# Attention scan and bilinear feed-forward on one core: pair 1's x, Wb's second piece and two first products change their places

## The chip, the cores and the metric
The kernel runs on one core of a Trainium2 chip. Five engines work side by side, each through its own list of instructions: TensorE (PE; its weight loads are shown as PEld), VectorE (DVE), ScalarE (ACT), GpSimd (POOL) and SyncE (SP). Transfers between memory and the on-chip buffer are issued by SP, ACT or GpSimd and carried by 16 DMA engines that all issuers share. The metric is the device time of one execution in microseconds (us), lower is better.

## The reference
First stage: for each of 4 batches x 8 heads a recurrent scan over 768 tokens, done in chunks of 32, with head size 32 and state size 16:

```
la  = log(clip(a)); cum = cumsum(la)              # in a chunk
M   = (C B^T) * exp(cum_i - cum_j) * causal
y   = M x  +  (C state) * exp(cum_i)
state = exp(sum la) * state + sum_j B_j x_j * exp(cum_last - cum_j)
```

Second stage, over the 3072 tokens with the heads side by side (256 wide):

```
out = ((y @ w_a) * (y @ w_b)) @ w_out             # w_a, w_b: 256 x 1536, w_out: 1536 x 256
```

Inputs and output are float32.

## The kernel before
The tokens of a batch are cut into 6 blocks of 128. A **pair** is one block of two batches, so there are 12 pairs; pairs 0 and 1 are the first block of all four batches. For a pair, B and C are scaled by decay factors (`scale_bc`), turned (`transposes`), and multiplied head by head (`scores`); the products are masked to the causal part (`mask`), x is scaled to float16 (`scale_x`), and `pv` or `pv_u` multiplies the masked products with x and so makes the scan's output y for this pair, laid into `X2T`. The feed-forward follows: products of `X2T` with Wa go to banks called `aps`, products with Wb to banks called `bps`, ACT copies `aps` out (`evac_a`), DVE multiplies both (`times`), and the product with Wo makes the output. Two pairs of the first blocks are done one after the other; later blocks take both pairs at once.

Wa and Wb are each 256 rows by 1536 columns. They are kept in two tiles by column half (index 0 and 1), and each tile has two pieces by row half, `f`. `load_w(W, t, f)` loads one piece; `load_w(W, t)` loads both. A GpSimd transfer turns float32 to float16 on its way. All weight loads are issued by GpSimd.

Every engine works its list strictly in the written order, since the kernel is scheduled by hand; semaphores for the data are put in by the framework. So the order of lines in the file is the order of each engine's work, and the order of a queue's issues is that of its transfers.

At the start, SP loads `a` and parts of pair 0's inputs, ACT other parts of them. GpSimd makes two masks by `affine_select`, then issues (L213 to L220) B and C of pair 1 in two halves each (`bt` 0 and 1), Wa's two pieces of columns 0, the second half of pair 1's x, and Wb's two pieces of columns 0. The first half of pair 1's x is issued by SP (L203) and held behind the reciprocal `f0` (L761, L762), so that it stays behind pair 0's x; the constant `c32` follows it on SP (L204).

From L757 on the compute: `warmup` products keep TensorE busy while data are on the way, DVE makes the decay factors of pair 0, TensorE its transposes and scores, DVE its four masked products. GpSimd scales B and C of pair 1 (L778, L783), then issues the second column halves of Wa and Wb (L784, L785), and makes `causal_q`, the mask for the later blocks (L786). On TensorE the order is: first half of pair 0's y (`pv_u(0, 0, ...)`, L792), the transposes of pair 1 (L795), second half of pair 0's y (L796), two first products with Wa of row half 0 (L801), the scores of pair 1 (L802), the other products of row half 0 (L804), those of row half 1 (L805), the products with Wb of row half 0 (L823), then `pv(1)` (L824) and the rest with Wb (L826, L827). ACT copies each half of pair 0's y out (`evac0`), the copies of row half 0 follow the first half, those of row half 1 the second. The helper `units_mm` (L625) holds the products with L628; its last arguments are the row half and which of the six products are done.

Psum banks are given out in the order of the calls of `bank` by the list `BANKS`; the first `aps` bank is one that nothing used before, the second and third are the two `py` banks of pair 0.

Of the kernel before, what the change touches and what calls it, by code (L numbers as in the profile page):

```python
# [14 lines left out]
ALU = mybir.AluOpType  # L15
PSUM = bass.MemoryType.PSUM
AFTER = mybir.DependencyInfo(mybir.DependencyClass.Sync, mybir.DependencyReason.DATA)
# [12 lines left out]
def kernel(  # L30
# [102 lines left out]
    def bank(name):  # L133
        return psf.tile([128, 512], f32, name=name, tag=f"ff{next(banks)}")
# [11 lines left out]
    def load1(eng, p, which, bt, i0=0, n=64):  # L146
        blk, bp = divmod(p, NBP)
        if p >= P0:
            return eng.dma_start(
                by_token(pair_in[p][which])[:, bt],  # L150
                (B, C, x)[which][2 * bp + bt, :, blk * Q : (blk + 1) * Q, :].rearrange("h q n -> q h n"),
            )
        src = (B, C, x)[which][2 * bp + bt, :, blk * Q + 2 * i0 : blk * Q + 2 * i0 + 2 * n, :]
        return eng.dma_start(
            pair_in[p][which][64 * bt + i0 : 64 * bt + i0 + n].rearrange("i h r n -> i h (r n)"),
            src.rearrange("h (i r) n -> i h (r n)", r=2),
        )
# [10 lines left out]
    def load_w(W, t, f=None):  # L168
        src = (moe_w_a if W is Wa else moe_w_b).rearrange("(f p) e -> p f e", p=128)[:, :, t * KC : (t + 1) * KC]
        fs = slice(0, 2) if f is None else slice(f, f + 1)  # L170
        return nc.gpsimd.dma_start(W[t][:, fs], src[:, fs])
# [28 lines left out]
    nc.vector.memset(hsx, 0.0)  # L200
    nc.vector.memset(causal_q, 1.0)
    nc.vector.memset(c32, 0.0)
    x1 = load1(nc.sync, 1, 2, 0)  # L203
    nc.sync.dma_start(c32[0:BH], p32_t.ap())  # L204
    nc.gpsimd.affine_select(
        out=ident, in_=ident, compare_op=ALU.is_equal, fill=0.0, base=0, pattern=[[-1, 128]], channel_multiplier=1
    )
# [7 lines left out]
            load1(nc.gpsimd, 1, w, bt)  # L215
    load_w(Wa, 0, 0)
    load_w(Wa, 0, 1)
    load1(nc.gpsimd, 1, 2, 1)
    load_w(Wb, 0, 0)
    load_w(Wb, 0, 1)  # L220

    def warmup(n, bank, reps=4):
        for _ in range(n):
# [83 lines left out]
    def scale_bc(p, which, eng, factor=None):  # L307
        blk, bp = divmod(p, NBP)
        name = ("bm", "cm")[which]
        if p >= P0:  # L310
            f = (fBl, fCl)[which][:, blk - P0 // NBP].rearrange("p (b t h) -> p b t h", b=NBP, t=2)[:, bp]
        else:
            f = (f_c(blk) if which else fB[:, blk])[:, :, bp]
        raw = by_token(pair_in[p][which]) if p >= P0 else pair_in[p][which].rearrange("p h r n -> p r h n")
        m_ = pre.tile([128, 2, H, N], f16, name=name, tag=name)
        eng.tensor_tensor(
            out=m_,
            in0=raw,
            in1=(f if factor is None else factor).unsqueeze(3).broadcast_to((128, 2, H, N)),
            op=ALU.mult,  # L320
        )
        st.setdefault(p, {})[name] = m_
    def transposes(p, ps=None, between=None, apart=False):
        s = st[p]
        if p >= P0:
            ps = [bank("tr").bitcast(f16)] * 2
            TB, TC = ps[0][:, 0:256], ps[0][:, 256:512]
            on_dve = False
        elif ps is None:
            ps = [bank("tb") if p == 1 else SC[0], SC[1]] if apart else None  # L330
            on_dve = apart
            TB, TC = (TT[:, 0:256], TT[:, 256:512]) if ps is None else [t_.bitcast(f16)[:, 0:256] for t_ in ps]
        else:
            on_dve = True
            TB, TC = [t_.bitcast(f16)[:, 0:256] for t_ in ps]
        BT = mid.tile([128, 2, 2, 2, 64], f16, name="bt", tag="bt")
        CT = mid.tile([128, 2, Q], f16, name="ct", tag="ct")
        b_ = []

        def turn(T_, src):  # L340
            for r in range(2):
                nc.tensor.transpose(T_[:, r * 128 : (r + 1) * 128], src[:, r].rearrange("p h n -> p (h n)"), ident)  # L342

        def copy_bt(e):
            o_ = BT[:, e].rearrange("p r t i -> p (r t i)")
            b_.append(nc.scalar.activation(out=o_, in_=TB, func=AF.Copy, scale=par[:, e : e + 1]))  # L346

        turn(TB, s["bm"])
        if between:
            between()  # L350
        turn(TC, s["cm"])
        copy_bt(0)
        copy_bt(1)
        if p >= P0:
            nc.scalar.copy(CT.rearrange("p t q -> p (t q)"), TC)
            s["BT"], s["CT"] = BT.rearrange("p e r t i -> p e r (t i)"), CT
            return
        c_ = (nc.vector.tensor_copy if on_dve else nc.scalar.copy)(
            CT.rearrange("p t (i r) -> p r (t i)", r=2), TC.rearrange("p (r c) -> p r c", r=2)
        )  # L360
        if apart:
            for i_ in b_:
                tc.declare_no_dep(c_.ins, i_.ins.name, reason="reads of two banks")
        s["BT"], s["CT"] = BT, CT
# [32 lines left out]
    def product(p, m):  # L397

        if p >= P0:
            return (  # L400
                st[p]["T1"][:, 2 * m : 2 * m + 2].rearrange("p e t q -> p (e t) q"),
                SC[m].rearrange("p (c q) -> p c q", q=Q),
                causal_q.unsqueeze(1).broadcast_to((128, 4, Q)),
            )
        return (
            st[p]["T1"][:, 2 * m : 2 * m + 2].rearrange("p e r q -> p e (r q)"),
            SC[m].rearrange("p (e c) -> p e c", e=2),
            causal.rearrange("p r q -> p (r q)").unsqueeze(1).broadcast_to((128, 2, 2 * Q)),
        )
# [9 lines left out]
    def mask(out_in, by_pool=False):  # L419
        o_, i_, c_ = out_in  # L420
        if by_pool:
            tmp = mid.tile([128, *c_.shape[1:]], f32, name="tmp", tag="tmp")
            nc.scalar.copy(tmp, i_)  # L423
            nc.gpsimd.tensor_tensor(out=o_, in0=tmp, in1=c_, op=ALU.mult)  # L424
        else:
            nc.vector.tensor_tensor(out=o_, in0=i_, in1=c_, op=ALU.mult)  # L426

    def pv_u(p, u, py, first):
        s = st[p]
        for bt, g in itertools.product(range(2), range(4)) if p >= P0 else ():  # L430
            c0 = 32 * (g ^ 2 * bt)
            nc.tensor.matmul(  # L432
                py[bt, u][c0 : c0 + 32],
                by_token(s["X16"])[:, bt, u * 4 + g],
                s["T1"][:, u * 4 + g, bt],
                start=False,
                stop=True,
                skip_group_check=True,
                tile_position=(0, c0),
            )  # L440
        for r in range(2) if p < P0 else ():
            for g in range(4):
                for bt in range(2):
                    h = u * 4 + g
                    k = slice(64 * bt, 64 * bt + 64)
                    c0 = 32 * g
                    nc.tensor.matmul(  # L447
                        py[bt][c0 : c0 + 32, u * Q : (u + 1) * Q],
                        s["X16"][k, h, r, :],
                        s["T1"][k, h, r, :],  # L450
                        start=(first and u == 0 and r == 0),
                        stop=(r == 1),
                        skip_group_check=True,
                        tile_position=(64 * bt, c0),
                    )
# [169 lines left out]
    def units_mm(p, k2s, W, ps, f, ks):  # L625
        for j in ks:
            k2, t_, kk = k2s[j // 2], ps[j // 2], j % 2
            nc.tensor.matmul(  # L628
                t_[:, kk * 2 * Q : (kk + 1) * 2 * Q],
                w_up(W, 2 * k2 + kk, f),  # L630
                X2T[:, p, :, f],
                start=(f == 0 and kk == 0),
                stop=(f == 1),
                skip_group_check=True,
            )
# [117 lines left out]
    def pull(p):  # L753
# [5 lines left out]
    over_mid(0, 1)  # L759
    first_factors()  # L760
    f0 = nc.vector.reciprocal(fB[:, 0, :, 0], f_c(0)[:, :, 0])  # L761
    tc.add_manual_dep(x1.ins, f0.ins.name, AFTER, reason="x of pair 1 behind x of pair 0")  # L762
    scale_bc(0, 0, nc.vector)
    scale_bc(0, 1, nc.vector)
    scan(1, 2)
# [15 lines left out]
    mask(product0(1, 0))  # L781
    mask(product0(1, 1))
    scale_bc(1, 1, nc.gpsimd)  # L783
    load_w(Wa, 1)  # L784
    load_w(Wb, 1)  # L785
    nc.gpsimd.affine_select(  # L786
        out=causal_q, in_=causal_q, compare_op=ALU.is_ge, fill=0.0, base=0, pattern=[[1, Q]], channel_multiplier=-1
    )
    warmup(4, tb)
    py = [bank("py0"), bank("py1")]  # L790

# [1 line left out]
    for bt in range(2):  # L793
        evac0(0, bt, nc.scalar, py)
    transposes(1, apart=True)  # L795
    pv_u(0, 1, py, True)  # L796
    for bt in range(2):
        evac0(1, bt, nc.scalar, py)
    scan(3, 5)
    aps = [bank("aps") for _ in range(3)]  # L800
    units_mm(0, range(3), Wa, aps, 0, range(2))  # L801
    scores(1)  # L802
    mask(product(1, 3), by_pool=True)
    units_mm(0, range(3), Wa, aps, 0, range(2, 6))  # L804
    units_mm(0, range(3), Wa, aps, 1, range(6))  # L805
    asb = [evac_a(aps[0])]
# [273 lines left out]
```

## Time and profile before

| | us |
|---|---|
| median of three runs | 125.06 (124.92 to 125.37) |
| the profiled execution | 125.11 |
| its span, first to last instruction | 123.4 |
| PE busy in the span | 117.3 (95%) |
| DVE busy | 91.0 (74%) |
| ACT busy | 75.7 (61%) |
| POOL busy | 61.2 (50%) |
| busy time of PE from 8.0 to 13.2 | 4.21 of 5.20 |
| share of the DMA engines from 8.0 to 13.2 | 1.14 (transfers overlap on an engine) |

The profile is of one execution, and its clock starts with the first instruction; what lies between span and time (1.7 us) is outside the instructions. In lines of the timeline the columns are start, duration, engine, line of the kernel, operation, what it writes from what, how many; in square brackets stands the idle time just before and what ended it. Several instructions of a kind are drawn together in one line, whose duration then runs from the first to the last. An issue of a transfer by GpSimd is shown with the time that GpSimd spends on it, not with the transfer's. Issue to landing, as medians: Wa's first two pieces 5.5 us, Wb's 6.4 us, x by GpSimd 5.8 us.

### The profile page before, as it was taken

The page shows a single profiled execution, that of the slowest core. Times are in us where ns is not written, and L with a number is a line of the kernel's source. Part 1 is how long each engine was busy: PE and PEld are TensorE (multiplying, and loading weights), DVE is VectorE, ACT ScalarE, POOL GpSimd, SP SyncE. Part 2 cuts the span into 40 slices and gives each one's busy share as a digit, 9 for nine tenths or more (in the row PEclk, how much of TensorE's full clock was granted, in tenths as well). Part 3 has the DMA queues.
Part 4 walks back from the last instruction along what each step waited for, and adds up shares of the span by engine and source line. Part 5 has one row for each costly group of instructions (what it writes and reads, how often), then busy time and mean ns, then how long its engine had stood idle before and what let it go on. Part 6 is the DMA issues. An engine that isn't in the chain of part 4 may idle for free.

```text
span 123.4 us, 3704 instructions
## 1 busy us (share of the span) xinstructions
PE 117.3 (95%) x1456; PEld 80.0 (65%) x1456; DVE 91.0 (74%) x182; ACT 75.7 (61%) x158; POOL 61.2 (50%) x88
## 2 busy tenths in 40 slices
PE   6799799999999999999999999999999999999990
PEld 2345669889898798744477465757464775555890
DVE  3999598973995979799986988996889544747200
ACT  0447846837669866987669767457637746657220
POOL 7997989099492994097996970056000000000000
PEclk9999999999999999999999999999999999999999
DMA  3999999978899989799977601011101012010122
GB/s 66 195 155 210 185 198 204 164 137 77 89 125 115 108 111 103 91 118 93 129 271 169 204 5 45 5 43 45 43 0 43 5 43 88 0 48 0 43 85 85
DMA packets 56401, 12.15 MB, mean 99 GB/s; under 512 B 51168, under 2 KB 55936, under 8 KB 56384
## 3 DMA queue, kind: packets, MB, share of 16 engines
q1 hardware_dynamic: 51808, 7.43, 36.3%
q0 software_dynamic: 2304, 4.06, 17.4%
q10 hardware_dynamic: 2272, 0.43, 1.8%
q8 instruction: 11, 0.18, 0.6%
q14 instruction: 6, 0.05, 0.1%
HBM read 11.13 MB, written 3.15 MB: 116 GB/s over the span
## 4 chain that ended last, share of the span: by engine, by line
PE 85%; DMA 7%; DVE 5%; issue 1%; ACT 0%; DVEq 0%
PE ops L718 17%; PE aps L693 17%; PE bps L693 16%; PE ops L661 9%; PE aps L615 8%; PE bps L615 7%; DMA Wb<-in_moe_w_b_dram 5%; PE SC L372 2%; PE SC L432 2%; PE tr L342 2%; DMA a_sb<-in_a_dram 2%; DVE hk L646 1%; PE bps L628 1%; PE SC L447 1%; PE SC L522 1%; DVE fC L246 1%
## 5 line engine op out<-in xcount | busy, mean ns | idle before, releaser
L639 ACT COPY asb<-aps 128x512 f32<-128x512 f32 x72 | 41.9, 587 | 16.0 <-PE aps L693 10.4
L703 DVE TENSOR_TENSOR hkb<-bps,asb 128x512 f16<-128x512 f32 x48 | 32.3, 688 | 11.8 <-ACT asb L639 10.4
L693 PE MATMUL aps<-XB,Wa 128*128 128x512 f16 x96 | 28.6, 379 | 0.0
L693 PE MATMUL bps<-XB,Wb 128*128 128x512 f16 x96 | 28.5, 379 | 0.0
L718 PE MATMUL ops<-Wo,hkb 128*128 128x256 f16 (+1 forms) x204 | 22.8, 267 | 0.0
L718 PEld LDWEIGHTS <-hkb 128*128 128x128 f16 x204 | 18.4, 98 | 3.0
L426 DVE TENSOR_TENSOR t<-SC,causal_q 128x512 f16<-128x512 f32 x27 | 17.3, 681 | 2.2 <-PE SC L372 2.2
L646 DVE TENSOR_TENSOR hk<-bps,asb 128x512 f16<-128x512 f32 x24 | 15.6, 681 | 3.5 <-ACT asb L639 2.1
L693 PEld LDWEIGHTS <-Wb 128*128 128x128 f16 x96 | 9.9, 103 | 11.0 <-issue 0.2
L693 PEld LDWEIGHTS <-Wa 128*128 128x128 f16 x96 | 9.7, 104 | 9.2 <-issue 0.3
L730 ACT ACTIVATE osb<-ops 128x256 f32<-128x256 f32 (+1 forms) x16 | 6.0, 376 | 12.7 <-PE ops L718 12.6
L615 PE MATMUL bps<-X2T,Wb 128*128 128x256 f16 x84 | 12.6, 273 | 0.1
L615 PE MATMUL aps<-X2T,Wa 128*128 128x256 f16 x84 | 12.5, 273 | 0.2 <-DVE hk L646 0.2
L305 POOL TENSOR_SCALAR x<-xn 128x512 f16<-128x512 f32 x8 | 11.9, 1489 | 0.7
L661 PE MATMUL ops<-Wo,hk 128*128 128x256 f16 x96 | 11.7, 273 | 0.0
L661 PEld LDWEIGHTS <-hk 128*128 128x128 f16 x96 | 9.0, 98 | 1.2
L615 PEld LDWEIGHTS <-Wb 128*128 128x128 f16 x84 | 8.5, 103 | 1.1 <-issue 0.5
L615 PEld LDWEIGHTS <-Wa 128*128 128x128 f16 x84 | 8.4, 104 | 1.2 <-issue 0.5
L424 POOL TENSOR_TENSOR t<-tmp,causal_q 128x512 f16<-128x512 f32 x5 | 5.8, 1156 | 6.2 <-ACT tmp L423 6.1
L426 DVE TENSOR_TENSOR t<-SC,causal 128x512 f16<-128x512 f32 x13 | 8.2, 678 | 0.3 <-PE SC L387 0.2
L595 POOL TENSOR_TENSOR spair<-U,ch 128x128 f16<-128x128 f32 x8 | 3.1, 398 | 10.3 <-DVE U L579 10.3
L346 ACT ACTIVATE bt<-tr,ch 128x256 f16<-128x256 f16 x16 | 6.7, 472 | 0.5 <-PE tr L342 0.5
(101 smaller groups left out, 136.1 us busy)
## 6 DMA issues: line engine op xcount, KB each, us to landing
out_dram<-osb SPq DMA_DIRECT2D x23, 128.0 KB, 1.8
xn<-in_x_dram SPq DMA_DIRECT2D x5, 256.0 KB, 4.6
cn<-in_C_dram SPq DMA_DIRECT2D x8, 128.0 KB, 4.3
bn<-in_B_dram SPq DMA_DIRECT2D x8, 128.0 KB, 4.7
Wo<-in_moe_w_out_dram POOLq DMA_DIRECT2D x2, 384.0 KB, 5.9
xn<-in_x_dram POOLq DMA_DIRECT2D x3, 256.0 KB, 4.8
Wa<-in_moe_w_a_dram POOLq DMA_DIRECT2D x2, 192.0 KB, 5.5
xn<-in_x_dram SPq DMA_DIRECT2D x3, 128.0 KB, 3.5
```

The lines of the kernel that those rows point to most:

```text
L305: eng.tensor_scalar(xo, xi, XS, None, ALU.mult)
L346: b_.append(nc.scalar.activation(out=o_, in_=TB, func=AF.Copy, scale=par[:, e : e + 1]))
L424: nc.gpsimd.tensor_tensor(out=o_, in0=tmp, in1=c_, op=ALU.mult)
L426: nc.vector.tensor_tensor(out=o_, in0=i_, in1=c_, op=ALU.mult)
L615: nc.tensor.matmul(ps[:, kk * 2 * Q : (kk + 1) * 2 * Q], w_up(W, k, f), X2T[:, p, :, f], start=(f == 0), stop=(f == 1), skip_group_check=True,
L639: (nc.vector.tensor_copy if on_dve else nc.scalar.copy)(asb, a_ps)
L646: nc.vector.tensor_tensor(out=s["hk"][:, 2 * k2 : 2 * k2 + 2, :].rearrange("p k q -> p (k q)"), in0=b_ps, in1=asb, op=ALU.mult)
L661: nc.tensor.matmul(o_ps[:, 0:d_model], hk[:, k, bt * Q : (bt + 1) * Q], Wo[:, k, :], start=(k == 0), stop=(k == NK - 1), skip_group_check= ...
L693: nc.tensor.matmul(t_, w_up(W, k, f), XB[:, blk - P0 // NBP, f].rearrange("p t j q -> p (t j q)"), start=(f == 0), stop=(f == 1), skip_gro ...
L703: return lambda: nc.vector.tensor_tensor(out=s["hk"][:, k], in0=ps[1], in1=asb, op=ALU.mult)
L718: nc.tensor.matmul(o_ps[:, 0:w], hk[:, k, c * Q : (c + 1) * Q], Wo[:, k, cs], start=(k == 0), stop=(k == NK - 1), skip_group_check=True,)
L730: nc.scalar.activation(out=o_sb[:, 0:w], in_=o_ps[:, 0:w], func=AF.Copy, scale=1.0 / (YS * YS))
```

## The change
Four moves. The first half of pair 1's x is issued by GpSimd behind the second, both behind Wa's pieces, in place of SP; the constant that follows it on SP now holds the dependency on `f0`. Wb's second piece is issued behind the scalings of pair 1. `causal_q` is made behind GpSimd's masked product of pair 1. The two first products with Wa stand ahead of the second half of pair 0's y, and only the first `aps` bank is taken there; the other two are taken behind the scores of pair 1.

```diff
-    x1 = load1(nc.sync, 1, 2, 0)
-    nc.sync.dma_start(c32[0:BH], p32_t.ap())
+    c1 = nc.sync.dma_start(c32[0:BH], p32_t.ap())
...
     load_w(Wa, 0, 0)
     load_w(Wa, 0, 1)
-    load1(nc.gpsimd, 1, 2, 1)
+    for bt in (1, 0):
+        load1(nc.gpsimd, 1, 2, bt)
     load_w(Wb, 0, 0)
-    load_w(Wb, 0, 1)
...
-    tc.add_manual_dep(x1.ins, f0.ins.name, AFTER, reason="x of pair 1 behind x of pair 0")
+    tc.add_manual_dep(c1.ins, f0.ins.name, AFTER, reason="constant behind x of pair 0")
...
     scale_bc(1, 1, nc.gpsimd)
+    load_w(Wb, 0, 1)
     load_w(Wa, 1)
     load_w(Wb, 1)
-    nc.gpsimd.affine_select(
-        out=causal_q, in_=causal_q, compare_op=ALU.is_ge, fill=0.0, base=0, pattern=[[1, Q]], channel_multiplier=-1
-    )
...
     transposes(1, apart=True)
+    aps = [bank("aps")]
+    units_mm(0, range(1), Wa, aps, 0, range(2))
     pv_u(0, 1, py, True)
     for bt in range(2):
         evac0(1, bt, nc.scalar, py)
     scan(3, 5)
-    aps = [bank("aps") for _ in range(3)]
-    units_mm(0, range(3), Wa, aps, 0, range(2))
     scores(1)
     mask(product(1, 3), by_pool=True)
+    nc.gpsimd.affine_select(
+        out=causal_q, in_=causal_q, compare_op=ALU.is_ge, fill=0.0, base=0, pattern=[[1, Q]], channel_multiplier=-1
+    )
+    aps += [bank("aps") for _ in range(2)]
     units_mm(0, range(3), Wa, aps, 0, range(2, 6))
```

## The prediction

> **What bounds the kernel now.** I read the page's chain first, then the chain in order of time over the first 45 us, then the timelines of TensorE, GpSimd (POOL) and ScalarE (ACT) around its odd pieces, and last the landings. On the page PE holds 85% of the chain, DMA 7%, DVE 5%. In order of time (columns: start us, us, what):
>
> ```profile
> 6.91 6.16 DMA Wb<-in_moe_w_b_dram
> 13.07 0.05 issue
> 13.12 0.62 PE bps L628 x4
> 13.73 0.35 PE SC L447 x32
> 14.08 0.31 PE SC L474 x32
> 14.39 0.56 PE bps L628 x4
> ...
> 15.05 0.69 DVE hk L646
> ...
> 16.85 0.60 PE aps L615 x4
> ```
>
> The reader is to see one transfer, the first piece of Wb (issued 6.91, landed 13.07), that releases TensorE, and behind it a chain that hardly leaves TensorE. The table of busy time by stretches gives PE 5.00 us of 17 to 22, 18.00 of 22 to 40, 29.94 of 40 to 70. So whatever moves the first Wb products, or the pair-1 block behind them, moves the end one for one; nothing later in the kernel is touched.
>
> TensorE before and behind that landing:
>
> ```profile
> 9.00 0.29 PE L342 MATMUL tb<-ident,bm 128*128 128x128 f16 x2
> 9.36 0.28 PE L342 MATMUL SC<-ident,cm 128*128 128x128 f16 x2
> 9.57 0.69 PE L447 MATMUL py<-t,x 64*32 64x128 f16 x16
> 10.24 0.40 PE L628 MATMUL aps<-X2T,Wa 128*128 128x256 f16 x2
> 10.57 0.43 PE L387 MATMUL SC<-ct,bt 32*64 32x128 f16 x32
> 10.93 1.47 PE L628 MATMUL aps<-X2T,Wa 128*128 128x256 f16 x10
> 13.12 0.62 PE L628 MATMUL bps<-X2T,Wb 128*128 128x256 f16 x4 [0.71 <-DMA Wb<-in_moe_w_b_dram]
> 13.66 0.42 PE L447 MATMUL SC<-t,x 64*32 64x128 f16 x32
> ```
>
> The sixteen products of pair 0's second half (9.57) take 0.69 us where the same sixteen of the first half took 0.39 at 8.68: about 0.3 us is waiting for the last mask of pair 0. And TensorE stands 0.71 us before 13.12. GpSimd, whose order of issue is the order of the transfers:
>
> ```profile
> 6.20 0.77 POOL L154 DMA_DIRECT2D xn<-in_x_dram  x1
> 6.91 1.13 POOL L171 DMA_DIRECT2D Wb<-in_moe_w_b_dram  x2
> 8.11 0.62 POOL L316 TENSOR_TENSOR bm<-bn,fB 128x256 f16<-128x256 f32 x1
> 8.69 0.61 POOL L316 TENSOR_TENSOR cm<-cn,fC 128x256 f16<-128x256 f32 x1
> 9.25 0.77 POOL L171 DMA_DIRECT2D Wa<-in_moe_w_a_dram  x1
> ```
>
> Issuing ends at 8.04, landing is at 13.07: the issue isn't what is late, the transfer queue is (DMA share 1.14 from 8 to 13.2 in the table of stretches).
>
> The semaphore events of the trace give each transfer's landing engine by engine (16 engines, each adds one). Wa's two pieces: last engine 10.20 and 11.52, last but one 9.62 and 11.02. Pair 1's x: the SP half 11.80, the GpSimd half 12.31 (last but one 10.47 and 11.34). Wb's pieces: 13.07 and 14.07 (last but one 12.30 and 13.16; the first engine 11.39 and 12.37). So one engine runs 0.6 to 1.0 us behind all others, and TensorE waits for that engine.
>
> **The change, part by part.**
>
> *x of pair 1, first half, from SP to GpSimd.* It removes one issue from SP (SP has nothing else to do until 21.6; the constant behind it now goes out at once behind f0, 5.24 for 5.86, and is needed at 16.02: nothing). It adds one issue to GpSimd, 0.72 us (two x issues in a row, 16.39, take 1.43). The bytes stay ahead of Wb's first piece in both kernels, so what counts is what this half costs the slowest engine. From that engine's packets: before, the SP half goes as 256-byte packets, one between two of Wa's, 142 ns a pair where Wa's packet alone took 135, then a burst of 17 in 0.24 us; with some eight more near 9.85 that is about 0.35 us in all. On the other engines its 32 packets take about 18 ns each, 0.58 us at most. In the GpSimd queue x goes as two packets of 4 KB an engine; x of pair 2, two in a row in that queue, landed 0.49 us apart (22.19, 22.68) and 0.37 to 0.58 behind Wo's piece. So it costs 0.37 to 0.58 in place of 0.30 to 0.58: between 0.2 saved and 0.3 lost. For the slowest engine I sum: Wa piece two 0.95 (first to second Wb piece of one engine, 0.95 in the packets), x 0.45, x 0.45, Wb piece one 0.95, together 2.80 behind Wa's first landing; measured before it was 13.07 - 10.20 = 2.87. Taken: **-0.07 us**, Wb at 13.00; Wa's second piece lands near 11.2 in place of 11.52.
> The Trainium skill, "DMA: Bandwidth & Descriptors", section "Queues, rings and completion order", has each engine take turns between queues at packet granularity. The 142 ns pairs agree with it; by that rule alone the SP half would be spread thin and cost Wa's first piece up to eight packets of 256 bytes, about 0.1 us, and the sum would be the same within that.
>
> *GpSimd's own order.* x 6.20, x 6.91, Wb piece one 7.63 to 8.20, then the scalings of pair 1 at 8.27 and 8.85 for 8.11 and 8.69: 0.16 later, as an x issue (0.72) is dearer than the Wb issue (0.57) that leaves. So the second transposes of pair 1 come at 9.52 for 9.36. Wb's second piece goes out at 9.46 for 7.48, Wa's and Wb's second halves at 10.03 and 10.79 for 9.25 and 10.01, done 11.52. The masked product by GpSimd that follows waits for ACT's copy anyway (end 11.71): covered, 0.2 us to spare. Wb's second piece: from issue to first packet a GpSimd transfer on idle engines took 1.9 us (2.21 to 4.10), so it can start by 11.4; the engines are then at Wb's first piece or just through it, the slowest until 12.75. It lands at about 14.0 as before and is needed at 14.3. If that cover were gone each us of lateness past 14.3 would cost one.
> *The constant mask* (0.31 us) moves from 10.74 to behind GpSimd's product: its first reader is pair 4 near 39.8. Behind it the issues of pair 2's B and C slip 0.3 us, as transfers they queue until 16.5 anyway; the stop before Wo's second half (18.30, for Wb's last landing, 18.02 plus the wake) takes up the 0.3. Nothing.
>
> *Two first products ahead of pair 0's second half.* No work is added. TensorE now waits in order for Wa's first piece: 10.20 if the late engine is late again. Before, 9.57 to 10.24 was half waiting, so the second half (masks ready 9.90, 0.35 us at full rate) ends near 10.8 instead of 10.25, its two copies on ACT end 11.25 for 10.77, the scores of pair 1 end 11.1 for 10.93, its masks on DVE 13.16 for 12.96, GpSimd's part 13.04 for 12.96, the first-half products 12.2 for 12.40. ACT's scaled x:
>
> ```profile
> 12.01 0.59 ACT L639 COPY asb<-aps 128x512 f32<-128x512 f32 x1 [0.29 <-PE aps L628]
> 12.49 0.63 ACT L303 ACTIVATE x<-xn 128x512 f16<-128x512 f32 x1
> 13.02 1.06 ACT L639 COPY asb<-aps 128x512 f32<-128x512 f32 x2
> ```
>
> It sits behind the copy of aps 0 in both kernels, near 12.4 to 13.1; x lands by 12.1. Pair 1's block (13.66) needs the masks, that x and four Wb products, which end at 13.00 + 0.55; the new latest of the others is 13.16. So this part costs nothing while Wa's first piece lands before about 10.6; what it would save is seen only if Wb comes first, and then pair 1's readiness is the next thing late, at 12.75 (Wa early) to 13.2.
>
> Sum: -0.07 on the chain. The profiled execution took 125.11 us (span 123.4 and 1.7 around it), 0.05 over the median of the three runs; 125.11 - 0.07 - 0.05 is **125.0**.
>
> **The rivals.**
>
> *The late engine is gone* (faster). It is late by one packet: begun at 9.02, it took 0.83 us, while no other packet of any engine stalled between 7.6 and 9.6. It fell where the SP half was in the queues. Without it Wb lands with the last but one engine, 12.30 or a little earlier, Wa at 9.6. Then the scores begin at 10.35, masks end at 12.75, x at 12.63, and pair 1's block begins at 12.85 for 13.66: -0.8, **124.3**; if only half is won, 124.6. Against: three runs lie within 0.45 us of each other and the profiled one in their middle, so a like delay is in all of them, and where it comes from the trace doesn't say.
>
> *The software queue makes the late engine later* (slower). Packets of x in GpSimd's queue stalled 0.63 and 0.64 us where they began (9.66, 9.78). If the late engine takes such a stall on the added half, its Wb piece lands at 13.65, the products follow, **125.7**; it decides from one stall of over 0.5 us there. For it: 4 KB packets in this queue have a median of 172 ns but took up to 1.26 us. Against: most don't stall.
> The Trainium skill, the same page, section "Latency and other measured facts", holds that two of the sixteen engines are usually slower and guesses at contention around the software descriptor rings. One persistently late engine in this trace fits; that the GpSimd queue is its cause no run here shows.
>
> *Wb's second piece is now too late* (slower). Issued 2 us later, it would have to land after 14.95 for 0.65 us of loss; the queue holds work until 12.75, so I give it little. 125.7 as well.
>
> *It does not do what it says*: if Wa's first piece still lands at 10.2, the two products don't fill the old gap but wait. That is in my sum.
>
> **Numbers.** A measurement of this kernel tells some 0.5%, 0.62 us, from no change. Queue-bound as summed: 0.50 (its own range 124.7 to 125.4, all within the bound but a twentieth on each side). Late engine gone: 0.27, two thirds of it past 124.43. Later still: 0.17, Wb's second piece 0.06, most of both past 125.68. Faster 0.22, same 0.56, slower 0.22. Leaving a tenth at each end: 124.2 to 125.8.
>
> **What would show it.** In the profile after: Wb's first landing near 13.0 and the wait of TensorE on it 0.7 to 0.9 us (right); under 12.5 with pair 1's block before 13.2 (first rival); over 13.5 (second); a wait on Wb before the second-half products near 14.3 (third). The two first products at 10.2, or earlier if Wa lands so; the scalings on GpSimd at 8.27. Wrong it would be if something past 17 us moved, which I hold untouched.

## The result and the profile after

The changed kernel takes 125.5 us (median; 124.87 to 126.98) where the kernel before takes 124.98 (124.48 to 126.62) on the same chips: a ratio of 1.0048, with a 95% interval of 1.0029 to 1.0068. It is slower by about 0.6 us; 125.0 was predicted. The profile that came with the result is of an execution of 126.98 us, the longest of them, which the comparison leaves out as disturbed; so it is read beside a second one of the same kernel, of 125.40 us (span 123.7), which stands 0.29 over the 125.11 of the profile before and is called the second profile from here on. In the changed kernel the lines below the change have numbers one lower: L627 is the L628 of before.

The chain in order of time, second profile (start us, us, what), answers to the first lines shown of before:

```profile
9.47 5.27 DMA Wb<-in_moe_w_b_dram
14.74 0.05 issue
14.79 0.41 PE bps L627 x2
```

The chain still hangs on a transfer of Wb, but on another: this one is issued at 9.47, not 6.91, and so is the second piece, and it releases the last six products with Wb, not the first four. The chain of the first profile has the same three steps, later:

```profile
9.47 6.12 DMA Wb<-in_moe_w_b_dram
15.60 0.05 issue
15.64 1.46 PE bps L627 x6
```

TensorE in the second profile (start, duration, engine, line, operation, what, how many, idle time before and what ended it):

```profile
9.70 0.38 PE L627 MATMUL aps<-X2T,Wa 128*128 128x256 f16 x2
10.01 0.32 PE L446 MATMUL py<-t,x 64*32 64x128 f16 x16
10.40 0.43 PE L386 MATMUL SC<-ct,bt 32*64 32x128 f16 x32
10.76 1.27 PE L627 MATMUL aps<-X2T,Wa 128*128 128x256 f16 x10
12.29 0.62 PE L627 MATMUL bps<-X2T,Wb 128*128 128x256 f16 x4 [0.25 <-DMA Wb<-in_moe_w_b_dram]
12.84 0.42 PE L446 MATMUL SC<-t,x 64*32 64x128 f16 x32
13.09 0.47 PE L473 MATMUL SC<-x,bm 64*32 64x64 f16 x32
13.49 0.40 PE L627 MATMUL bps<-X2T,Wb 128*128 128x256 f16 x2
14.79 0.84 PE L627 MATMUL bps<-X2T,Wb 128*128 128x256 f16 x6 [0.90 <-DMA Wb<-in_moe_w_b_dram]
15.46 0.60 PE L614 MATMUL aps<-X2T,Wa 128*128 128x256 f16 x4
```

The change does what it says: the two first products at 9.70 leave the sixteen of pair 0's second half only 0.32 us to take (0.69 before). The first piece of Wb lands early, the wait on it is 0.25 instead of 0.71, and pair 1's block starts at 12.84, 0.82 ahead of before. Then TensorE stands 0.90 us for the second piece, which cost no wait before:

```profile
14.32 1.05 PE L628 MATMUL bps<-X2T,Wb 128*128 128x256 f16 x8
15.21 0.60 PE L615 MATMUL aps<-X2T,Wa 128*128 128x256 f16 x4
```

The 0.82 gained and more are gone: the next products, pair 1's first with Wa (L615), start at 15.46 where they started at 15.21, 0.25 later, beside 0.29 in the time.

The same place in the first profile:

```profile
13.49 0.40 PE L627 MATMUL bps<-X2T,Wb 128*128 128x256 f16 x2
15.64 1.46 PE L627 MATMUL bps<-X2T,Wb 128*128 128x256 f16 x6 [1.75 <-DMA Wb<-in_moe_w_b_dram]
16.90 1.06 PE L614 MATMUL aps<-X2T,Wa 128*128 128x256 f16 x4
```

The wait is 1.75 us, and behind it four products take 1.06 us that took 0.60 above: TensorE ran at half its clock from 15.35 to 18.76 (last section). They start 1.69 us later than before, and the time is 1.87 over that of the profile before.

GpSimd in the first profile, whose order of issue is that of the transfers:

```profile
6.20 1.49 POOL L154 DMA_DIRECT2D xn<-in_x_dram  x2
7.60 0.66 POOL L171 DMA_DIRECT2D Wb<-in_moe_w_b_dram  x1
8.33 0.62 POOL L315 TENSOR_TENSOR bm<-bn,fB 128x256 f16<-128x256 f32 x1
8.91 0.61 POOL L315 TENSOR_TENSOR cm<-cn,fC 128x256 f16<-128x256 f32 x1
9.47 0.59 POOL L171 DMA_DIRECT2D Wb<-in_moe_w_b_dram  x1
```

That order came as forecast, to 0.06 us. What did not is when the second piece lands. By the semaphore events of the trace the last of the 16 engines lands Wb's first and second piece at 13.07 and 14.07 before, 1.00 apart; at 12.24 and 14.74 in the second profile, 2.50 apart; at 12.19 and 15.60 in the first, 3.41 apart. "DMA: Bandwidth & Descriptors" of the Trainium skill, section "Why a DMA increments its semaphore by 16 and not by 1", says that the engines finish independently and that only the full 16 means landed. The trace agrees: in the second profile fourteen engines had landed the second piece by 13.28, in time for TensorE, which was ready at 13.89; the last two landed it at 14.28 and 14.74. In the first profile fifteen had by 14.44, the last at 15.60. TensorE waits for one or two engines of the sixteen.

What the transfers moved from 11.0 to 14.5 us (busy time of PE, PEld, DVE, ACT and POOL with instruction counts; then the granted clock, the DMA share and GB/s), before and then the second profile:

```profile
11.00:14.50 3.50, 2.77 (x81) 1.91 (x81) 2.69 (x6) 2.98 (x6) 2.76 (x5) 1.00 1.13 188
```

```profile
11.00:14.50 3.50, 2.64 (x80) 1.78 (x77) 2.63 (x6) 3.41 (x7) 3.36 (x5) 1.00 0.93 146
```

The last column falls from 188 to 146 GB/s: 42 x 3.5 us is 147 KB less. The share falls too, from 1.13 to 0.93, and by the transfer records GpSimd's queue had 17.7 packets under way on average from 12 to 14 us before and 14.1 here, fewer than there are engines. That alone isn't the reason for the wait: the five profiles of the changed kernel, three of them with another edit, have 13.8 to 17.3 by the same count, and the late issue alone, which cost no such wait, has 14.8 and 14.0.

### The profile page after: what moved, and what is told of

Its sections match the earlier page's. It is cut to its first block, busy times and chain, and to the rows that moved or that the text cites. A ratio compares the mean times of both kernels' runs of the same rounds, so it can differ in the third digit from the quotient of the medians.

```text
span 125.3 us, 3704 instructions
## 1 busy us (share of the span) xinstructions
PE 118.6 (95%) x1456; PEld 80.8 (65%) x1456; DVE 91.2 (73%) x182; ACT 75.6 (60%) x158; POOL 62.0 (50%) x89
## 4 chain that ended last, share of the span: by engine, by line
PE 85%; DMA 7%; DVE 4%; POOL 2%; issue 1%; ACT 0%; DVEq 0%; POOLq 0%
PE ops L717 17%; PE aps L692 17%; PE bps L692 16%; PE ops L660 9%; PE aps L614 8%; PE bps L614 8%; DMA Wb<-in_moe_w_b_dram 5%; PE SC L371 2%; PE SC L431 2%; DMA a_sb<-in_a_dram 2%; PE tr L341 2%; PE bps L627 1%; PE SC L521 1%; DVE fC L245 1%; PE SC L386 1%
## 5 line engine op out<-in xcount | busy, mean ns | idle before, releaser
L425 DVE TENSOR_TENSOR t<-SC,causal_q 128x512 f16<-128x512 f32 x27 | 17.3, 680 | 2.2 <-PE SC L371 2.2
L729 ACT ACTIVATE osb<-ops 128x256 f32<-128x256 f32 (+1 forms) x16 | 6.0, 376 | 12.7 <-PE ops L717 12.6
L614 PE MATMUL aps<-X2T,Wa 128*128 128x256 f16 x84 | 13.0, 281 | 0.0
```

The lines of the kernel that those rows point to most:

```text
L614: nc.tensor.matmul(ps[:, kk * 2 * Q : (kk + 1) * 2 * Q], w_up(W, k, f), X2T[:, p, :, f], start=(f == 0), stop=(f == 1), skip_group_check=True,
L729: nc.scalar.activation(out=o_sb[:, 0:w], in_=o_ps[:, 0:w], func=AF.Copy, scale=1.0 / (YS * YS))
```

## The experiments

Theory A: Wb's second piece, issued behind the scalings, lands late and TensorE waits for it (the prediction's third rival). Its rivals in the expectations: B, x makes GpSimd's queue slower as a whole, and Wb's first piece lands at 13 or later; C, the loss is the lowered clock alone; F, a fetch of TensorE's instructions makes one engine late. A2 is A narrowed to the case that both transfer moves meet. All ratios are against the kernel before on the same chip, with 95% intervals. None is more than 0.5% from no change, so what each profile shows counts beside the time; there is one profile of each kernel, and two of the changed kernel and of the late issue alone.

**The changed kernel again.**

> The changed kernel itself, for a second profile of it. Theory A (Wb's second piece, issued 2 us later, finds the transfer queue run dry and lands late): the wait on Wb's second piece behind the first two row-half-0 products of the third bank is there again, 0.5 us or more, with Wb's first piece landed before 12.6. Theory B (x in GpSimd's queue makes the queue slower as a whole): Wb's first piece lands at 13 or later. Theory C (the loss is a lowered granted clock alone): no wait over 0.5 us on Wb's second piece, and a granted clock under 1 between 13 and 22. Ratio 1.003 to 1.007.

1.0032 (1.0002 to 1.0062), the second profile above: the wait on the second piece is there, at a clock of 1.0 throughout. So the loss is not only that of the clock (C). Wb's first piece landed at 12.24, so B's sign is not there either.

**The changed kernel, second piece back in its old place.**

```diff
     load_w(Wb, 0, 0)
+    load_w(Wb, 0, 1)
...
     scale_bc(1, 1, nc.gpsimd)
-    load_w(Wb, 0, 1)
```

> The changed kernel with one part undone: Wb's second piece issued right behind its first again, ahead of the scalings of pair 1, which then start 0.57 us later. Theory A: Wb's second piece lands about 1.0 us behind the first (near 13.2), no wait on it, and the kernel is faster than the one before: 124.3 to 124.7, ratio 0.994 to 0.998; pair 1's block then waits for its masks, near 13.1 to 13.4. Theory B: it stays as slow as the changed kernel, 1.003 or more. Theory C: as A for the time, as the pause is gone.

1.0022 (1.0002 to 1.0042): the gain expected isn't there. The pieces land 0.94 apart and the wait on the second is gone, as A has it. But the scalings now come 0.57 later, and the first piece's last engine at 13.40, 1.25 behind the last but one:

```profile
10.14 0.29 PE L342 MATMUL SC<-ident,cm 128*128 128x128 f16 x2 [0.29 <-POOL cm L316]
13.45 0.62 PE L628 MATMUL bps<-X2T,Wb 128*128 128x256 f16 x4 [0.84 <-DMA Wb<-in_moe_w_b_dram]
```

Undoing the late issue trades one wait for another. The best of its times is 124.88, that of before in the same runs 124.50. By time alone this kernel isn't told from the changed one (1.0032, 1.0002 to 1.0062): that the wait is gone is seen in the profile only.

**Each part alone, in the kernel before.** The late issue:

```diff
     load_w(Wb, 0, 0)
-    load_w(Wb, 0, 1)
...
     scale_bc(1, 1, nc.gpsimd)
+    load_w(Wb, 0, 1)
```

> The kernel before with this part alone: Wb's second piece issued behind the scalings of pair 1. Theory A: slower, by as much as the second piece lands past 14.3; the slow engine is busy with piece one until 12.8 here, so less than in the changed kernel: 0.2 to 0.8 us, ratio 1.002 to 1.006. Theory B: no change, 0.998 to 1.002.

> Once more the kernel before with the late issue of Wb's second piece alone. Theory A2: the second piece's last engine 1.0 to 1.6 us behind the first's as in the first look (1.54), no wait of TensorE on it over 0.3 us; ratio 0.998 to 1.003. If the late issue costs by itself: 1.003 or more.

1.0019 (0.9988 to 1.0050), and run again 1.0003 (0.9973 to 1.0033). The pieces land 1.54 and 1.57 apart, and TensorE shows no idle time before the second; in the second run its first product with that piece starts some 0.1 us late, at its landing (14.14). In the first of the two TensorE is 0.65 us ahead of before by 16.20 (the products at 16.85 there):

```profile
16.20 0.60 PE L614 MATMUL aps<-X2T,Wa 128*128 128x256 f16 x4 [0.32 <-DVE hk L645]
```

The lead is given back at pair 2's transposes; the timeline of each, in this order:

```profile
21.54 0.28 PE L341 MATMUL SC<-ident,cm 128*128 128x128 f16 x2 [0.56 <-POOL cm L315]
```

```profile
21.88 0.28 PE L341 MATMUL SC<-ident,cm 128*128 128x128 f16 x2 [0.61 <-POOL cm L315]
```

TensorE came early and waited for GpSimd's scaling instead. So the late issue alone shows no loss, and a lead of 0.65 us at 16.20 brought nothing in this profile.

The x halves alone:

```diff
-    x1 = load1(nc.sync, 1, 2, 0)
-    nc.sync.dma_start(c32[0:BH], p32_t.ap())
+    c1 = nc.sync.dma_start(c32[0:BH], p32_t.ap())
...
-    load1(nc.gpsimd, 1, 2, 1)
+    for bt in (1, 0):
+        load1(nc.gpsimd, 1, 2, bt)
...
-    tc.add_manual_dep(x1.ins, f0.ins.name, AFTER, reason="x of pair 1 behind x of pair 0")
+    tc.add_manual_dep(c1.ins, f0.ins.name, AFTER, reason="constant behind x of pair 0")
```

> The kernel before with this part alone: both halves of pair 1's x by GpSimd behind Wa. Both pieces of Wb are issued ahead of the scalings, which start 0.7 us later. Theory A: Wb's pieces land near 12.2 and 13.2 as the first did in the changed kernel; pair 1's block near 13.3, bound by its masks: faster by 0.3 us, ratio 0.996 to 0.999. Theory B: slower, 1.002 or more, with Wb's first piece at 13.0 or later.

1.0013 (0.9989 to 1.0036), expected faster. Alone, the added issue stands ahead of the scalings, which come 0.78 us later, and the first piece's last engine lands at 13.88, 1.07 behind the last but one. TensorE waits 1.32 for it:

```profile
13.92 0.62 PE L628 MATMUL bps<-X2T,Wb 128*128 128x256 f16 x4 [1.32 <-DMA Wb<-in_moe_w_b_dram]
15.12 1.06 PE L628 MATMUL bps<-X2T,Wb 128*128 128x256 f16 x8
```

The eight products behind wait for nothing: the pieces are 0.95 apart. Here too one engine is late, with no part of x on SP. B's sign, the first piece at 13 or later, is thus seen here and with the second piece back in its place (13.40), and in the kernel before as well (13.07), but in no profile that has the late issue.

The two first products alone (their lines of the diff, nothing else):

> The kernel before with this part alone: the two first products with Wa ahead of pair 0's second half. Transfers are as before. All theories: no change, ratio 0.998 to 1.002; the two products start near 9.7 to 10.2 and the scores of pair 1 within 0.3 us of before.

0.9992 (0.9968 to 1.0016): it costs nothing, as summed.

**Both transfer moves without the two first products.**

```diff
-    aps = [bank("aps")]
-    units_mm(0, range(1), Wa, aps, 0, range(2))
     pv_u(0, 1, py, True)
...
     scan(3, 5)
+    aps = [bank("aps") for _ in range(3)]
+    units_mm(0, range(3), Wa, aps, 0, range(2))
     scores(1)
...
-    aps += [bank("aps") for _ in range(2)]
```

> The change without its TensorE part: x by GpSimd and Wb's second piece behind the scalings, the first products in their old place. Theory A2 (the second piece is late only where both parts meet: with x in GpSimd's own queue the first piece is through early, and the second, issued late, follows 2.5 us behind it instead of 1.0): last engine of the second piece 2.3 to 3.4 us behind the last of the first, a wait of 0.7 us or more, ratio 1.002 to 1.006. If it takes all three parts: ratio 0.999 to 1.001.

1.0018 (0.9992 to 1.0044). The pieces land 1.78 apart, and there is a wait on the second, a short one:

```profile
14.41 0.83 PE L627 MATMUL bps<-X2T,Wb 128*128 128x256 f16 x6 [0.18 <-DMA Wb<-in_moe_w_b_dram]
```

That lies between what A and its rival gave. With the two first products the distance is 2.5 to 3.4 in five profiles; whether their place has a part in it, or this one profile fell well, isn't told apart.

**How long the second piece may wait.** Between the two scalings, 0.6 us earlier than in the change:

```diff
     scale_bc(1, 0, nc.gpsimd)
+    load_w(Wb, 0, 1)
...
     scale_bc(1, 1, nc.gpsimd)
-    load_w(Wb, 0, 1)
```

> The changed kernel with Wb's second piece issued between the two scalings of pair 1 (0.6 us earlier than in the change, and only the second scaling 0.6 us later). Theory A (the queue runs dry): the second piece lands on all but the slowest engine by 13.6, half-way between the change (14.3) and the kernel with that part undone (13.1); time between the two, ratio 1.000 to 1.003. Theory F (TensorE's instruction fetch, one packet of 16 KB that keeps one engine for 1 us, makes the last engine late wherever it falls): the last engine is 0.4 to 1.5 us behind the last but one on whichever transfer the fetch meets.

1.0026 (0.9994 to 1.0059). It lands at 13.43, 0.94 behind the first, and no product with Wb waits:

```profile
10.19 0.29 PE L341 MATMUL SC<-ident,cm 128*128 128x128 f16 x2 [0.48 <-POOL cm L315]
...
12.54 0.73 PE L627 MATMUL bps<-X2T,Wb 128*128 128x256 f16 x4
...
14.11 1.05 PE L627 MATMUL bps<-X2T,Wb 128*128 128x256 f16 x8
```

The price is again the second scaling, for which TensorE waits 0.48. Best time 124.92, before 124.57. And 0.23 us later than in the change, with the making of `causal_q` put ahead of the issue:

```diff
     scale_bc(1, 1, nc.gpsimd)
+    nc.gpsimd.affine_select(out=causal_q, ...)
     load_w(Wb, 0, 1)
...
-    nc.gpsimd.affine_select(out=causal_q, ...)
```

> The changed kernel with a larger dose of its one suspected part: the mask for the later blocks (0.3 to 0.45 us of GpSimd) stands ahead of Wb's second piece again, so that this piece is issued that much later still (9.8 to 9.9 for 9.47). Theory A (the late issue of the second piece costs): it lands and the kernel ends 0.3 to 0.5 us later than in the change: median 125.7 to 126.0, ratio 1.006 to 1.010. Theory F (a late engine from the fetch, whatever the issue): as the change, 1.003 to 1.005.

1.0043 (1.0017 to 1.0068), wait 0.95, landed 14.78: the same as the change. The growing loss that A expected isn't there; 0.23 us is little beside the spread of the landing (14.74 to 15.60).

**Is it TensorE's own instructions?** The transfer records show packets of 16 KB in an instruction queue; I take them for TensorE's (last section). The one near Wb's pieces runs from 11.50 to 12.94 in the second profile and from 12.32 to 13.37 in the first; in the profile before it ran from 13.78 to 14.74. More warm-up products should move that fetch.

```diff
-    warmup(11, SC[3])
+    warmup(44, SC[3], 1)
```

> The changed kernel with the eleven opening warm-up products of 512 columns cut into 44 of 128: the same columns, 66 more instructions on TensorE, so that its first fetch of 16 KB should come some 66 instructions sooner, near 9 us, ahead of Wb's pieces. Theory F: the fetch is over before 10.5; no engine is more than 0.5 us behind the last but one on Wb's second piece; the times over 125.8 are gone and the median falls to 124.8 to 125.1, ratio 0.999 to 1.001. Theory A alone: the second piece still lands at 14.3 or later, ratio 1.003 as in the changed kernel.

In the changed kernel: 1.0042 (1.0011 to 1.0073). The second piece is as late as ever, landed 15.48, wait 1.36. But the fetch begins at 11.08, not near 9, so it still lies among Wb's pieces, and this run doesn't take F away. It suggests that the fetch isn't the whole of it: the last engine landed 3.36 us behind the end of the fetch (12.12), and a piece takes some 0.95 on an engine. In the kernel before (`warmup(22, SC[3], 2)` for the same line):

> The kernel before with the eleven opening warm-up products of 512 columns cut into 22 of 256: 22 more instructions on TensorE. Theory F: the first fetch moves from 13.8 to 11 to 12.5, where Wb's pieces are under way, and one of them is late by 0.5 us or more on one engine: slower, ratio 1.001 to 1.004. Theory A: no change, 0.998 to 1.001.

1.0035 (1.0011 to 1.0060), with both pieces on time (12.62, 13.58) though the fetch ran from 12.73 to 13.68. What it lost shows in the timeline, in the last section.

Over all eighteen profiles F stays a rival. In six of them the last engine lands a piece of Wb 1.3 to 1.7 us behind the fourteenth (four of the changed kernel, two of them with another edit, and two of kernels with x in GpSimd's queue and the second piece ahead of the scalings), and in all six the fetch begins between 11.1 and 12.3. It begins in that stretch in two more, with 0.45 and 0.47. In the other ten it begins at 12.6 or later, and no last engine is more than 0.96 behind. So an engine that late came only with an early fetch. All eight profiles with the early fetch have x in GpSimd's queue, and no run has parted the two.

**Pair 1's block ahead of all products with Wb**, so that Wb is needed later. In the kernel before, and there once more with the issue of Wo's second half moved behind the second scaling of pair 2:

```diff
-    bps = [bank("bps") for _ in range(3)]
-    units_mm(0, range(3), Wb, bps, 0, range(4))
     pv(1, DS=(0, SC[:2]))
     ds_mm(0, 64, SC[:2])
-    units_mm(0, range(3), Wb, bps, 0, range(4, 6))
+    bps = [bank("bps") for _ in range(3)]
+    units_mm(0, range(3), Wb, bps, 0, range(6))
```

> The kernel before with one move on TensorE: pair 1's block ahead of all products with Wb, which then have 0.65 us more to land. If the landing of Wb's pieces (12.1 to 13.1, and 13.6 to 14.1) is what spreads the runs of the kernel before from 124.5 to 125.4, the spread shrinks and the median falls to 124.5 to 124.8, ratio 0.996 to 0.999. If pair 1's block is what is late, no change.

> The kernel of the line above with Wo's second half issued behind the scalings of pair 2 instead of ahead of them, so that these scalings no longer stand behind the landing of Wb's second half (18.0 before, 18.9 to 19.5 where x is in GpSimd's queue). If that stop is the next bound (TensorE waited 0.56 us for it in the kernel with Wb's second piece alone moved), another 0.1 to 0.4 us: 124.2 to 124.6, ratio 0.993 to 0.998. If Wo then lands late, a wait on Wo near 27 and a loss.

1.0013 (0.9993 to 1.0033) and 1.0006 (0.9986 to 1.0027): no gain. In the changed kernel, with all of Wb ahead of the scalings:

> The changed kernel with Wb's two pieces in one transfer (one issue of 0.73 us in place of two of 0.57) ahead of the scalings, and on TensorE pair 1's block ahead of all products with Wb. Theory A: Wb lands whole near 13.2, behind the start of pair 1's block near 13.0; no wait of TensorE over 0.3 us: 124.3 to 124.7, ratio 0.994 to 0.998. Theory F: the late engine makes Wb land at 14.0 to 14.5, a wait of 0.4 to 0.9 us: 124.7 to 125.2.

1.0050 (1.0025 to 1.0074), a miss: TensorE now waits for the masks of pair 1 and then for Wb still:

```profile
13.10 0.42 PE L446 MATMUL SC<-t,x 64*32 64x128 f16 x32 [0.77 <-DVE t L425]
...
14.31 1.49 PE L627 MATMUL bps<-X2T,Wb 128*128 128x256 f16 x12 [0.49 <-DMA Wb<-in_moe_w_b_dram]
```

The four Wb products had filled the time in which DVE finishes the masks. Wb, all of it issued at 7.60, landed at 14.27, no sooner than the second piece before (14.07).

**Is it GpSimd's later stop?** With the change, Wb's second column half lands at 18.9 to 19.5 for 18.02, and GpSimd stops 1.10 us (second profile) ahead of Wo's second half, for 0.48. `load_wo(1)` behind `scale_bc(2, 1, nc.gpsimd)` takes that stop away from the scalings, in the changed kernel and in that with the two first products alone:

> The changed kernel with the same move of Wo's second half. If the loss of the change lay at GpSimd's second stop (1.1 to 1.25 us in its two profiles, 0.48 before), the loss goes: ratio 0.999 to 1.001. Theory A2: it stays, 1.003 to 1.005, as the wait on Wb's second piece stays.

> The kernel before with the two first products ahead and with Wo's second half issued behind the scalings of pair 2, which then don't stand behind the landing of Wb's second half. If that stop gives back what comes early ahead of it: 124.3 to 124.7, ratio 0.995 to 0.999. If not: 0.999 to 1.001.

1.0049 (1.0024 to 1.0075): the loss stays, and so does the wait on the second piece, 0.93. And 0.9991 (0.9969 to 1.0013): no gain. The later stop isn't the cause.

**The runs by one measure.** GB/s from 11.0 to 14.5, the distance between the landings of Wb's two pieces at the fourteenth and at the last engine, and the wait of TensorE on the second piece (the kernel with all of Wb in one transfer has no such pair):

| what is moved | GB/s | fourteenth apart, us | last apart, us | wait, us | ratios |
|---|---|---|---|---|---|
| no transfer (before, two first products, more warm-up, pair 1 first, Wo's second half) | 182 to 204 | 0.84 to 0.97 | 0.95 to 1.01 | 0 | 0.9991 to 1.0035 |
| second piece alone (two runs) | 164, 149 | 0.99, 1.44 | 1.54, 1.57 | 0 | 1.0019, 1.0003 |
| x in GpSimd's queue, second piece ahead of a scaling (three kernels) | 162 to 169 | 0.98 to 1.01 | 0.94 to 0.95 | 0 | 1.0013 to 1.0026 |
| both, without the two first products | 161 | 1.59 | 1.78 | 0.18 | 1.0018 |
| the whole change (five profiles, three of them with another edit) | 145 to 154 | 1.10 to 2.37 | 2.50 to 3.41 | 0.90 to 1.75 | 1.0032 to 1.0049 |

The first row's 1.0035 is that of the added warm-up, with a cause of its own. Only the last row has the long distance and the long wait, and no kernel in it is free of a loss. The ratios by themselves don't part the last three rows, as their intervals overlap; the waits on the second piece do. The rate alone doesn't decide: one run of the second piece alone has 149 GB/s as well, with no wait. What sets the last row apart are its last engines. None of the runs made a version clearly faster than the kernel before.

## Why the prediction was wrong

*The step that failed* is the one that cost Wb's second piece at nothing: "it can start by 11.4; the engines are then at Wb's first piece or just through it, the slowest until 12.75. It lands at about 14.0 as before". The issue was forecast well (9.46, measured 9.47), and TensorE was ready for it at 13.89, so that the piece was needed 0.4 us sooner than forecast. The landing missed by more: 14.74 and 15.60 for 14.0. Two assumptions are in that step. One took the late engine of the profile before as given, and so the first piece's end at 13.0; it ended at 12.2. The other took the second piece to follow each engine's first by the usual 0.95, whenever it is issued while some engine still has work. For most engines that was nearly so (the fourteenth 1.18 behind in the second profile, but 1.94 in the first); the last came 2.50 and 3.41 behind. Before, the two pieces stood in the queue together, and the last engine was late on both alike (0.77 and 0.91 behind the last but one), so that the lateness fell out of their distance; issued apart, the second piece had a lateness of its own (0.05 on the first piece and 0.46 on the second in the second profile, 0.14 and 1.16 in the first).

*The sum's -0.07* on x was near nothing, and not what decided. By the chances as stated, the faster side comes to 0.205 (two thirds of 0.27 and a twentieth of 0.50), not 0.22; nothing hangs on it. *First rival*: its mechanism came, with the first piece landed at 12.24 for its 12.30 and pair 1's block at 12.84 for 12.85. Its gain did not: it took the second piece as on time. *Third rival*: this is what happened, at the place it named, and I gave it 0.06 on the ground that "the queue holds work until 12.75". It asked for a landing past 14.95 to lose 0.65; the second profile lost 0.29 at 14.74. The fault was to price the two rivals apart: where the first piece is early, TensorE is ready for the second sooner (13.89 for 14.3), and the work that was to cover its issue is gone sooner too.

*"Moves the end one for one"* is wrong in the direction of a gain: the late issue alone put TensorE 0.65 us ahead at 16.20, and it stood 0.56 for GpSimd at 21.54. With it goes the claim that nothing past 17 us moves. In the direction of a loss it held: 0.25 late at 15.46 beside 0.29 in the time.

*Second rival*: not on the first piece of the change, which was early, but its kind of lateness on the second. With the second piece ahead of a scaling it was on the first, whose last engine came 1.25 and 1.07 behind the last but one in two of the three kernels with x in GpSimd's queue; 0.77 in the profile before, 0.04 and 0.51 with the late issue alone. It comes and goes from one kernel's profile to the next.

*Right*: GpSimd's order (8.33, 8.91, 9.47 for 8.27, 8.85, 9.46), no price for the constant mask, and none for the two first products (0.9992). Wa's first piece landed at 9.40, so that they had not to wait for 10.2.

What the runs show is that the second piece landed late and TensorE stood 0.90 to 1.75 us for it in all five profiles of the changed kernel, three of them with another edit, and that a wait on this piece showed as idle time only where the late issue and x in GpSimd's queue were together (0.18 without the two first products). They don't show why the last engines take so long there; that stays open. A queue run dry was not tried apart from the late issue, and the packets under way don't part the kernels; the early fetch of instructions was not tried apart from x in GpSimd's queue. Nor do the runs show in which execution an engine is late, or how much of the loss the two first products have.

## What to carry to other kernels

Before a transfer is issued later, compare the last engine's landing, not the typical one, with its first use, and leave room for a lateness that it used to share with the transfer ahead of it (here the landings came 2.5 us and more apart in place of 1.0). When a change brings one piece in sooner, the next becomes the one that is waited for, so price the two together. And on an issuing engine that also computes, a place freed for one step is taken from another (an issue of 0.57 us moved the scalings by 0.57), so undoing the harmful part need not bring the gain back.

## What the runs showed of the hardware

*A pause halved the clock.* The clock row of the first profile's page has one slice at half, and cutting its stretch finer (columns as in the stretches above) shows when:

```profile
PEclk9999959999999999999999999999999999999998
```

```profile
15.00:15.25 0.25, 0.00 (x0) 0.00 (x0) 0.00 (x0) 0.00 (x0) 0.25 (x2) 1.00 0.80 111
15.25:15.50 0.25, 0.00 (x0) 0.00 (x0) 0.00 (x0) 0.00 (x0) 0.25 (x2) 0.70 0.93 154
...
18.50:18.75 0.25, 0.25 (x3) 0.19 (x2) 0.25 (x2) 0.08 (x1) 0.00 (x0) 0.50 1.08 215
18.75:19.00 0.25, 0.25 (x4) 0.21 (x3) 0.25 (x2) 0.00 (x0) 0.00 (x0) 0.97 1.23 217
```

A mean of 0.70 in a quarter microsecond puts the drop at 15.35, one of 0.97 the return at 18.76: 3.41 us at half. The trace's clock records have the clock rise to full at 5.11, so 10.24 us, three times 3.413, lie between rise and drop; in fourteen other profiles rise and last drop lie 119.47 us apart, 35 times 3.413. So the windows can be counted from the rise. In the one ahead of this drop (11.94 to 15.35) TensorE was busy for 1.76 of 3.41 us. Counted so in all sixteen profiles with such records, every window with 1.76 or less was followed by half the clock, those behind the last work included, and none with 1.90 or more. A wait of 0.90 (second profile) left 2.26; one of 1.36, longer than that, fell on both sides of a boundary at 15.05 and left 2.37 and 2.48, and the clock stayed at 1.0. "TensorE: Matmul & The Clock Gate" of the Trainium skill, Part 1, "What's actually happening", has a free-running window of 3413 ns and the lower clock after an idle one. The 3.41 us agree; but the window ahead of the drop was not idle but about half busy, and here that was enough.

*TensorE seems to stand for its own instructions.* With 22 more warm-up instructions ahead in the kernel before, TensorE stood in a new place, with nothing that the profile shows to wait for:

```profile
13.87 0.40 PE L628 MATMUL bps<-X2T,Wb 128*128 128x256 f16 x2
15.00 0.84 PE L628 MATMUL bps<-X2T,Wb 128*128 128x256 f16 x6 [0.73 <-issue]
```

Of the 16 KB packets in the instruction queue the first near this place ends at 13.68, 1.32 us ahead of the restart; in the kernel before it ends at 14.74 and TensorE restarts at 16.17, 1.43 us later, 22 instructions further on in the work. In four other kernels the distance is 1.33 to 1.38, and in all six the stop stands behind the same number of matmuls, 223. That it is the fetch that TensorE waits for is inferred from this. It is worth knowing for one thing: with 22 instructions more among the warm-up products a stop moved to where TensorE stood 0.73 us, and the kernel was 0.35% slower.
